# A tile split into two compact pieces, each with its own load and store, in a kernel that gates an image by channel

## The chip, the cores and the metric

One core of one Trainium2 chip. The metric is the device time of one execution in microseconds, median over runs. The kernel before takes 528.1 us.

## The reference

```python
def reference(x, w1d):                       # x: 1 x 384 x 384 x 384 bf16, w1d: 1 value
    g = jnp.einsum("bhwc->bc", x) / (H * W)  # mean of each channel over the image
    ...                                      # k = 1: the "convolution" is s = g * w1d[0]
    s = _sigmoid(s)
    return x * s[:, None, None, :]
```

The output needs the mean of all of x before its first element is certain, yet reading x twice would cost half as much again. The kernel therefore guesses: it takes the gate from 512 of the 147,456 positions, writes x times that gate, sums everything on the way, and at the end compares the true gate with the guess bit by bit in bf16. Only if they differ is everything done again. With the data of this case they don't.

## The kernel before

x is seen as 1152 rows of 128 positions x 384 channels (98.3 KB each), in 18 tiles of 64 rows. Four tiles fit in SBUF (`SLOTS` = 4). All loads of the first four tiles are issued at once; tile k + 4 is loaded into the place of tile k when tile k's store is done. Loads go out on the SyncE queue (except half of tile 0 and all of tile 2), stores on the ScalarE queue. Code cut to what the change touches:

```python
TILE, SLOTS, EARLY, LEAD, FORE, OWN = 64, 4, 4, 8, 32, 16

def dram(view, r0, n):      # n rows of 128 positions; partition p holds n neighbouring positions
    return view[r0 * P : (r0 + n) * P, :].rearrange("(p t) c -> p (t c)", p=P)

# in load: columns i..i+m of an n-row tile
plan.dma(queue, at(place + i, m), dram(x_rows, r0, n)[:, i * C : (i + m) * C], ...)

load(0, TILE, 0, hi=LEAD)                           # 8 rows of tile 0 first: the guess needs 4
plan.dma("sync", w_one[0:1, 0:1], w1d.unsqueeze(0), writes=["w_one"])
load(0, TILE, 0, ("sync", "scalar"), lo=LEAD)       # the other 56 rows, 28 on each queue
load(slot(1), TILE, row0(1))
load(slot(2), TILE, row0(2), ("scalar", "scalar"))
load(slot(3), TILE, row0(3))
# ... sum_early, s_early, TensorE's sums ...
for k in range(n_tiles):
    if k >= SLOTS:
        for i in range(2) if k == SLOTS else () if k < SLOTS + 2 else (k - SLOTS,):
            sum_own(i)                              # VectorE sums 16 of the 64 rows itself
            put(slot(i), TILE, row0(i), parts=None if i else (FORE, TILE - FORE))
        if k == SLOTS:
            pause(slot(k))                          # 3.1 us of ScalarE, behind tile 0's store
        load(slot(k), TILE, row0(k), reads=["pause"] if k == SLOTS else ())
```

Since a tile's partition p holds 64 neighbouring positions, the 8 rows loaded ahead are 128 runs of 6,144 bytes, one every 49,152 bytes of DRAM. `put` gates in place on VectorE (tile 0 in two halves of 32 rows) and then issues one store.

## Time and profile before

| | before |
|---|---|
| median of runs | 528.11 us (527.96 to 529.07) |
| profiled execution | span 526.5 us |
| bytes | 113.25 MB read, 113.25 MB written |
| DMA engines, 10 to 520 us | share 1.00, 434 GB/s |
| VectorE | busy 84% of the span |
| issue of tile 0's store, of tile 1's store, of tile 4's load | 44.1, 68.6, 79.2 us |

A packet is one run of bytes that one DMA engine moves in one piece; each DMA ends with a completion packet of a few bytes on each of the 16 engines (those "under 512 B" below). "Share" is the time that the packets of a stretch took, over the stretch on all 16 engines, so 1.00 means that none was idle. The views count a packet whole in the stretch in which it starts. So over a few microseconds the share swings about 1. "Landing" is the time from the issue of a DMA to its completion.

### The profile page before, as it was taken

To read this page: it belongs to the slowest core of one execution; us is meant where nothing else is said; L and a number is where in the kernel's file an instruction comes from. 1 tells how busy PE (TensorE), PEld (TensorE's weight loads), DVE (VectorE), ACT (ScalarE), POOL (GpSimd) and SP (SyncE) were. 2 spreads that over 40 slices of the span, in tenths; PEclk is the share of its full clock that TensorE was granted. 3 is DMA by queue.
4 is the path that set the end of the run, shared out by engine and by line. 5 is a ranking of instruction groups with operands and counts; after the bars stand their busy time and mean duration, and the time that the engine had idled before them with its cause. 6 is when DMAs were issued, how large, how long until landed. Compare 5 with 4: busy or idle time off the path is not lost.

```text
span 526.5 us, 902 instructions
## 1 busy us (share of the span) xinstructions
PE 180.0 (34%) x648; PEld 0.2 (0%) x2; DVE 440.0 (84%) x78; ACT 5.8 (1%) x5; POOL 0.3 (0%) x6
## 2 busy tenths in 40 slices
PE   2255752043240707061422506070513315070701
PEld 0000000000000000000000000000000000000000
DVE  1869999999996978969696969789696969698795
ACT  1000020000000000000000000000000000000000
POOL 0000000000000000000000000000000000000000
PEclk9996967558585858567575858576675858585765
DMA  9999999999999999999999999999999999999998
GB/s 375 433 459 405 418 448 448 418 418 467 429 418 418 467 429 418 429 459 426 418 429 459 426 418 441 445 429 418 448 437 429 418 459 429 426 418 459 429 426 359
DMA packets 5620, 226.51 MB, mean 430 GB/s; under 512 B 626, under 2 KB 626, under 8 KB 754
## 3 DMA queue, kind: packets, MB, share of 16 engines
q10 hardware_dynamic: 3024, 122.29, 53.7%
q1 hardware_dynamic: 2594, 104.20, 46.0%
q14 instruction: 2, 0.02, 0.0%
HBM read 113.25 MB, written 113.25 MB: 430 GB/s over the span
## 4 chain that ended last, share of the span: by engine, by line
DMA 42%; another core or an unknown queue 27%; DVE 21%; issue 7%; SPq 0%; ACT 0%; DVEq 0%
DMA arena<-in_x_dram 24%; DMA out_dram<-arena 18%; DVE part L338 12%; DVE arena L210 7%; DVE own L345 1%; DVE total L326 0%; SPq L109 0%; DVE own L363 0%; DVE terms L356 0%; ACT arena L488 0%; DVE total L496 0%; DVE total L482 0%; DVE wrong L504 0%; DVE total L324 0%
## 5 line engine op out<-in xcount | busy, mean ns | idle before, releaser
L248 PE MATMUL acc<-arena,ones 128*128 128x512 bf16 x637 | 176.1, 441 | 312.2 <-PEq L292 310.8
L210 DVE TENSOR_TENSOR arena<-arena,s_early 128x24576 bf16<-128x24576 bf16 (+1 forms) x19 | 233.2, 12278 | 11.5 <-PE acc L248 6.5
L338 DVE TENSOR_REDUCE part<-arena 128x384 f32<-128x6144 bf16 x17 | 179.2, 10539 | 56.9 <-DMA arena<-in_x_dram 56.9
L338 DVE TENSOR_REDUCE own<-arena 128x384 f32<-128x6144 bf16 x1 | 10.4, 10435 | 0.6 <-DMA arena<-in_x_dram 0.6
L345 DVE TENSOR_TENSOR own<-own,part 128x384 f32<-128x384 f32 x17 | 9.5, 558 | 0.6
L425 DVE TENSOR_SCALAR w_scaled<-w_all 128x1 f32<-128x1 f32 x2 | 0.2, 152 | 8.0 <-PE w_all L416 8.0
L248 PE MATMUL acc_own<-terms,ones 128*128 128x384 bf16 x3 | 1.4, 479 | 15.3 <-DVE terms L356 15.3
L488 ACT ACTIVATE arena<-total,w_scaled 128x384 bf16<-128x384 f32 x1 | 0.6, 615 | 440.3 <-DVE total L482 440.3
L326 DVE TENSOR_TENSOR total<-total,acc 128x128 f32<-128x128 f32 (+2 forms) x10 | 3.9, 393 | 0.3
L399 ACT ACTIVATE arena<-warm 128x3456 bf16<-128x3456 f32 x1 | 3.1, 3082 | 61.9 <-DMA out_dram<-arena 61.9
L416 PE MATMUL w_all<-w_one,ones 1*128 1x1 bf16 x1 | 0.2, 158 | 9.3 <-DMA w_one<-in_w1d_dram 9.3
L248 PE MATMUL acc<-zeros,ones 128*128 128x512 bf16 x6 | 2.3, 507 | 0.0
L324 DVE COPY total<-acc 128x384 f32<-128x384 f32 x2 | 1.1, 554 | 1.2 <-PE acc L248 1.2
L410 ACT ACT_TABLE_LOAD x1 | 1.3, 1283 | 2.3 <-issue 2.3
L433 DVE MEMSET ones<- 128x128 bf16 x1 | 0.2, 165 | 1.3 <-PEq L611 1.3
L363 DVE TENSOR_TENSOR own<-own,terms 128x384 f32<-128x384 f32 x2 | 1.1, 559 | 0.1
L356 DVE CAST terms<-own 128x384 bf16<-128x384 f32 x3 | 1.1, 359 | 0.1
L496 DVE TENSOR_TENSOR total<-arena,s_early 128x384 f32<-128x384 uint16 x1 | 0.6, 558 | 0.7 <-ACT arena L488 0.7
L448 ACT ACTIVATE s_early<-total,w_scaled 128x384 bf16<-128x384 f32 x1 | 0.6, 614 | 9.8 <-DVE total L326 9.8
L482 DVE TENSOR_TENSOR total<-total,acc_own 128x384 f32<-128x384 f32 x1 | 0.6, 554 | 0.1
L246 PE MATMUL acc<-arena,ones 128*128 128x512 bf16 x1 | 0.6, 608 | 0.0
L504 DVE TENSOR_REDUCE wrong<-total 128x1 f32<-128x384 f32 x1 | 0.6, 553 | 0.0
(10 smaller groups left out, 1.2 us busy)
## 6 DMA issues: line engine op xcount, KB each, us to landing
out_dram<-arena ACTq DMA_DIRECT2D x18, 6144.0 KB, 49.9
arena<-in_x_dram SPq DMA_DIRECT2D x16, 6144.0 KB, 41.8
arena<-in_x_dram ACTq DMA_DIRECT2D x2, 3072.0 KB, 41.5
arena<-in_x_dram ACTq DMA_DIRECT2D x1, 2688.0 KB, 14.0
arena<-in_x_dram SPq DMA_DIRECT2D x1, 2688.0 KB, 21.4
arena<-in_x_dram SPq DMA_DIRECT2D x1, 768.0 KB, 7.8
w_one<-in_w1d_dram SPq DMA_DIRECT2D x1, 0.0 KB
```

Source lines behind the costliest of these rows:

```text
L210: return lambda e: e.tensor_tensor(to_v, v, s_b, ALU.mult)
L246: loaded.append(e.matmul(bank, weights, moving, start=start, stop=stop))
L248: return e.add_instruction(mybir.InstMatmult(name=nc.get_next_instruction_name(), engine=mybir.EngineType.PE, ins=[e.lower_ap(moving), e.l ...
L324: emit = lambda e, part=part, of=of: e.tensor_copy(part, of)
L326: emit = lambda e, part=part, of=of: e.tensor_tensor(part, part, of, ALU.add)
L338: lambda e: e.reduce_sum(to[:], view, axis=mybir.AxisListType.X),
L345: lambda e: e.tensor_tensor(own[:], own[:], part[:], ALU.add),
L356: lambda e, term=term: e.tensor_copy(term, own[:]),
L363: lambda e, term=term: e.tensor_tensor(own[:], own[:], term, ALU.subtract),
L399: lambda e: e.activation(to, warm[:, 0:1].broadcast_to([P, PAUSE * C]), ACT_F.Sigmoid),
L410: lambda e: e.activation(warm[:, 1:2], warm[:, 0:1], ACT_F.Sigmoid),
L448: lambda e: e.activation(s_early[:], total[:], ACT_F.Sigmoid, scale=w_scaled[:, 0:1]),
```

## The change

The intent, as its code suggests: let the first 8 rows be a small tile of their own, contiguous in DRAM (runs of 6,144 bytes that follow each other), which can be loaded alone and, once gated, stored alone, ahead of the other 56 rows. The pause then waits for the last row of tile 0 instead of the first. Cut to its core:

```diff
-    load(0, TILE, 0, hi=LEAD)
+    load(0, LEAD, 0)
     plan.dma("sync", w_one[0:1, 0:1], w1d.unsqueeze(0), writes=["w_one"])
-    load(0, TILE, 0, ("sync", "scalar"), lo=LEAD)
+    load(LEAD, TILE - LEAD, LEAD, ("sync", "scalar"))
...
+    def put_first():
+
+        gated(0, FORE, 0)
+        store(0, LEAD, 0)
+        gated(FORE, TILE - FORE, FORE)
+        store(LEAD, TILE - LEAD, LEAD)
...
-                put(slot(i), TILE, row0(i), parts=None if i else (FORE, TILE - FORE))
+                put(i) if i else put_first()
             if k == SLOTS:
-                pause(slot(k))
+                pause(slot(k) + TILE - 1)
```

(The rest splits `put` into `gated` and `store` and drops two parameters of `load`.)

More of the change, by code (lines that the diff above doesn't have):

```diff
@@ L227, in bass_standalone__channel_attn_eca__vision_kernel, with load @@
     plan = Planner(nc, "a", 70)
-    def load(place, n, r0, queues=("sync",), lo=0, hi=None, reads=()):
-        i, hi = lo, hi or n
-        for queue, m in zip(queues, split(hi - lo, -(-(hi - lo) // len(queues)))):
+    def load(place, n, r0, queues=("sync",), reads=()):
+        i = 0
+        for queue, m in zip(queues, split(n, -(-n // len(queues)))):
             plan.dma(
@@ L378, in join_own, with gated, store, put @@
             )
-    def put(place, n, r0, to=None, parts=None):
-        to, i = place if to is None else to, 0
-        for m in parts or [n]:
-            plan.op(
-                "vector",
-                gate(to + i, place + i, m, s_early),
-                reads=["s_early"] + rows(place + i, m),
-                writes=rows(to + i, m),
-            )
-            i += m
+    def gated(place, n, to):
+        plan.op(
+            "vector",
+            gate(to, place, n, s_early),
+            reads=["s_early"] + rows(place, n),
+            writes=rows(to, n),
+        )
+    def store(place, n, r0):
         plan.final.append(
-            plan.dma("scalar", dram(o_rows, r0, n), at(to, n), reads=rows(to, n))
+            plan.dma("scalar", dram(o_rows, r0, n), at(place, n), reads=rows(place, n))
         )
+    def put(k, to=None):
+        to = slot(k) if to is None else to
+        gated(slot(k), TILE, to)
+        store(to, TILE, row0(k))
+    def put_first():
[3 more added lines that the diff above has]
+        store(LEAD, TILE - LEAD, LEAD)
     def pause(r0):
@@ L471, in bass_standalone__channel_attn_eca__vision_kernel @@
         sum_own(k)
-        put(slot(k), TILE, row0(k))
-    put(slot(last), TILE, row0(last), slot(n_tiles))
+        put(k)
+    put(last, slot(n_tiles))
     sum_own(last)
```

## The prediction

> **What bounds the kernel now.** I read the head of the page and its DMA rows first, because this kernel reads x once and writes it once and does little else.
>
> ```profile
> span 526.5 us, 902 instructions
> PE 180.0 (34%) x648; PEld 0.2 (0%) x2; DVE 440.0 (84%) x78; ACT 5.8 (1%) x5; POOL 0.3 (0%) x6
> ...
> DMA  9999999999999999999999999999999999999998
> ...
> DMA packets 5620, 226.51 MB, mean 430 GB/s; under 512 B 626, under 2 KB 626, under 8 KB 754
> ...
> q10 hardware_dynamic: 3024, 122.29, 53.7%
> q1 hardware_dynamic: 2594, 104.20, 46.0%
> ```
>
> The reader is to see three things. The DMA digit is 9 in every slice but the last. VectorE is busy 84%, a high number, but not a full one. And the two queues split the bytes unevenly: q10 carries the 113.25 MB of stores plus 9.04 MB of early loads (28 rows of tile 0 and the 64 rows of tile 2; one row is 128 x 384 x 2 bytes, 98.3 KB), so q10 is the ScalarE queue and q1 the SyncE queue.
>
> Next I asked for the busy time by stretch, to find the places where the DMA engines are not full:
>
> ```profile
> core 0: us, PE busy (x) PEld busy (x) DVE busy (x) ACT busy (x) POOL busy (x), PEclk, DMA share, GB/s
> 0.00:1.00 1.00, 0.00 (x0) 0.00 (x0) 0.00 (x0) 0.00 (x0) 0.20 (x4) 1.00 0.07 6
> 1.00:2.00 1.00, 0.00 (x0) 0.00 (x0) 0.17 (x1) 0.00 (x0) 0.13 (x2) 1.00 1.07 184
> ...
> 523.00:524.00 1.00, 0.00 (x0) 0.00 (x0) 0.00 (x0) 0.00 (x0) 0.00 (x0) 0.50 1.13 492
> 524.00:525.00 1.00, 0.00 (x0) 0.00 (x0) 0.00 (x0) 0.00 (x0) 0.00 (x0) 0.50 0.15 57
> 525.00:526.00 1.00, 0.00 (x0) 0.00 (x0) 0.00 (x0) 0.00 (x0) 0.00 (x0) 0.50 0.00 0
> ...
> 10.00:520.00 510.00, 179.24 (x646) 0.00 (x0) 438.35 (x72) 4.24 (x3) 0.00 (x0) 0.70 1.00 434
> ```
>
> From 10 to 520 us the engines move 434 GB/s at a share of 1.00. Data starts about 1.3 us into the span and stops at about 524.2 us. So the time is 1.3 us of start, 226.5 MB at 433 GB/s, which is 523.1 us, and some 2.2 us of end: 526.6 against the 526.5 measured. There is no other term. In such a kernel a change helps only if it removes bytes, raises the rate, shortens those 3.5 us, or closes a hole; and it hurts only if it opens one.
>
> Last I read the stretch that the change touches, in the timeline:
>
> ```profile
> 13.61 0.61 ACT L448 ACTIVATE s_early<-total,w_scaled 128x384 bf16<-128x384 f32 x1 [9.82 <-DVE total L326]
> ...
> 31.08 13.03 DVE L210 TENSOR_TENSOR arena<-arena,s_early 128x12288 bf16<-128x12288 bf16 x2 [6.45 <-PE acc L248]
> 44.14 0.36 ACTq L109 DMA_DIRECT2D out_dram<-arena  x1
> ...
> 68.44 10.50 DVE L338 TENSOR_REDUCE part<-arena 128x384 f32<-128x6144 bf16 x1
> ...
> 76.09 3.08 ACT L399 ACTIVATE arena<-warm 128x3456 bf16<-128x3456 f32 x1 [61.87 <-DMA out_dram<-arena]
> ...
> 79.19 0.33 SPq L109 DMA_DIRECT2D arena<-in_x_dram  x1
> ```
>
> Tile 0 is gated in two halves (6.55 us each) from 31.08 us, when TensorE has summed its first 32 rows, to 44.1; its one store is issued there. Tile 1's store follows at 68.6. Tile 0's store is reported at 76.09, the ScalarE pause runs, and SyncE issues the load of tile 4 at 79.19.
>
> **What the Trainium skill says.** All four places are on the page "DMA: Bandwidth & Descriptors". (1) "Where 436 GB/s comes from" gives a fabric ceiling of 435.2 GB/s; the trace agrees, 434 GB/s over 510 us is at it. (2) "Queues, rings and completion order" says that each DMA engine goes round its queues packet by packet, so a queue's share follows its packet size. The trace agrees: from 37.6 to 44.1 us the two queues have 48 and 49 packets, but 1.57 and 1.20 MB. So does the first 8-row load: alternating with 21,504-byte packets it should need 8 packets per engine x (6,144 + 21,504) bytes at 433/16 = 27.06 GB/s, 8.2 us, and lands 7.8 us after issue. (3) "Latency and other measured facts" warns of row pitches at large powers of two; the pitches here are 49,152 bytes before and 6,144 and 43,008 after, none a power of two, and the first stretch already runs near full rate. (4) "Anatomy of one DMA" puts some 2 us of fixed cost per DMA on confirming the write; it fits the 2.2 us at the end here, and the change doesn't touch the last store.
>
> **The change part by part.** *The loads.* Same three pieces of 8, 28 and 28 rows on the same queues, same bytes per partition and packet, only with another pitch in DRAM. From 2 to 10 us the kernel before moves 421 GB/s, so at most 8 x 12/433 = 0.2 us is to be had from a better pattern. The small piece also feeds the early sum, but the first gate waits for TensorE at 31.08 us, and s_early is there at 14.2; a microsecond there buys nothing. Worth: 0 to -0.2 us.
>
> *The data in the early sum.* The 512 positions sampled for s_early are others. If the early gate differed from the true one in any bf16 bit, everything would be done again. I computed both from the inputs: the weight is 0.0012, and the sigmoid stays within 2.1e-6 of 0.5 for the old sample and for the new one, and every value rounds to exactly 0.5 in bf16. No second pass.
>
> *The stores.* One DMA is added: 128 packets of 6,144 bytes and 16 completion packets, while tile 0's other 128 packets shrink to 43,008 bytes; bytes are unchanged. Packets go from 5620 to 5764. The 8-row store is issued after the first gate, at 31.08 + 6.55 = 37.6 us instead of 44.1. It does not start then: the ScalarE queue still holds tile 2's second half, which lands 41.5 us after its issue, so at about 43. Then it alternates with tile 3's load on the SyncE queue, 49,152-byte packets: 8 x (6,144 + 49,152) bytes / 27.06 GB/s = 16.3 us. An 8-row store that alone would take 1.8 us thus ends near 60 us, some 22 us after issue, and the 56-row store waits behind it.
>
> That looks bad for tile 0, but in the same 16.3 us the load gets 8 packets per engine, which is all of tile 3. So tile 3 lands near 62 us instead of at 72, and the 56-row store then has the engines to itself: 5.5 MB / 433 GB/s = 12.7 us. Together: all work issued by 44.1 us is four tiles of loads and one of stores, 31.46 MB, which at 433 GB/s from 1.3 us ends at 74.0 in either order; plus the report, 76, where the trace has 76.09. So the pause and the load of tile 4 stay at 76 and 79 us, within 1 us. The tile that comes early, tile 3, is gated only at 127 us.
>
> *The pause.* It waits for the 56-row store instead of the 64-row one: the same event. Sum of all parts: -0.2 to +0.2 us on 526.5.
>
> **The rivals.** *A hole opens.* If the DMA ran dry before tile 1's store at 68.6 us, the loss would be the gap. For it: VectorE paces the stores there, one each 23.9 us. Against: the work on hand at 68.6 lasts to 74.0, 5.4 us of margin, in any order. Later, one tile's load and store occupy the engines for 29.05 us, a slot's round of four tiles is 116 us, and alone its load, sum, gate and store would need 14.5 + 24 + 14.5 = 53 us; 63 us of slack. At the end the last store takes 21.5 us from its issue at 502.9 to 524.4 or so, 14.5 of them its own: 7 us of backlog. This rival would need to delay something by over 5 us and would make 529 to 533. *The small store helps.* Writes that start 6.5 us sooner could bring everything forward by as much, giving 522 to 526. Against: the engines are full between 37.6 and 44.1, so bytes only change places; and at 435.2 GB/s the bytes alone take 520.5 us, so over 0.8% is out of reach. *A different pattern moves the rate*, by compact loads or small writes: it bears on 1.6 MB, 3.6 us of engine time, so even a 20% change is 0.7 us. *A second pass* would make about 1050 us; the arithmetic above rules it out.
>
> **Range and chances.** The launch adds about 1.5 us to the span, and three runs of the kernel before lie between 527.96 and 529.07. With no net effect, I take its median, 528.1. The range is the spread of the runs plus about 1 us for a shift of phase that I can't work out: 526.9 to 529.4. Chances: faster by over 2% (under 517.5) is beyond the ceiling, 0.005; slower by over 2% needs 10 us of holes, 0.01; within 2%, 0.985.
>
> **What would show it right or wrong.** Right: DMA digits still all 9 and 434 GB/s in the middle, 5764 packets, 8-row store issued near 37.6 us and landing 20 to 25 us later, TensorE's sum of tile 3 starting near 62 us instead of at 72.3, the pause at 76 and tile 4's load at 79, each within 1 us, last data 524 us. Wrong: a stretch under 400 GB/s over 10 us anywhere before the end, tile 1's store issued after the engines ran dry, or a last load landing later than 490 us with the final store standing alone.

## The result, and the profile after

The changed kernel takes 528.23 us (528.13 to 528.59, 6 runs) against 528.12 us (527.90 to 529.07, 6 runs): a ratio of 1.0001, 95% interval 0.9988 to 1.0014. Ratios here are the mean time of one kernel's fast runs over that of the other's fast runs of the same rounds, so they are not quite the ratios of the medians quoted. The change did nothing that can be measured.

The page of the changed kernel, span, DMA share and rate in 40 slices, packets and queues:

```profile
span 527.1 us, 918 instructions
...
DMA  9999999999999999999999999999999999999997
...
DMA packets 5764, 226.51 MB, mean 430 GB/s; under 512 B 642, under 2 KB 642, under 8 KB 898
...
q10 hardware_dynamic: 3168, 122.29, 53.7%
q1 hardware_dynamic: 2594, 104.20, 45.9%
```

Packets go up by the 144 foretold, all on the ScalarE queue (q10: 3024 to 3168); bytes, mean rate and the row of nines stay. Busy time by stretch of the changed kernel, the last two columns being DMA share and GB/s:

```profile
2.00:10.00 8.00, 1.29 (x4) 0.20 (x2) 0.22 (x2) 1.49 (x2) 0.00 (x0) 1.00 1.04 431
10.00:520.00 510.00, 179.43 (x658) 0.00 (x0) 438.21 (x72) 3.70 (x2) 0.00 (x0) 0.68 1.00 433
```

What moved is inside the first 80 us. The timeline of the changed kernel (start, duration, engine, instruction, and in brackets the idle time before it and what ended it):

```profile
29.26 13.03 DVE L210 TENSOR_TENSOR arena<-arena,s_early 128x12288 bf16<-128x12288 bf16 x2 [4.82 <-PE acc L248]
35.85 32.48 ACTq L109 DMA_DIRECT2D out_dram<-arena  x3
...
63.01 7.93 PE L248 MATMUL acc<-arena,ones 128*128 128x512 bf16 x36 [0.63 <-PEq L292]
67.88 10.48 DVE L338 TENSOR_REDUCE part<-arena 128x384 f32<-128x6144 bf16 x1
67.99 0.34 ACTq L109 DMA_DIRECT2D out_dram<-arena  x1
76.50 3.08 ACT L410 ACTIVATE arena<-warm 128x3456 bf16<-128x3456 f32 x1 [62.86 <-DMA out_dram<-arena]
...
79.61 0.33 SPq L109 DMA_DIRECT2D arena<-in_x_dram  x1
```

In the kernel before, TensorE's sum of tile 3 is this line:

```profile
72.28 9.93 PE L248 MATMUL acc<-arena,ones 128*128 128x512 bf16 x35 [9.78 <-PEq L292]
```

The 8-row store is issued at 35.85 us, 8.3 us ahead of the old store. TensorE sums tile 3 from 63.01 us instead of from 72.28. But the pause still starts at 76.5 (76.09 before) and tile 4's load goes out at 79.6 (79.19). Where the early store's head start went is in the list of DMA issues (KB each, us from issue to landing), changed kernel:

```profile
out_dram<-arena ACTq DMA_DIRECT2D x1, 5376.0 KB, 34.2
...
out_dram<-arena ACTq DMA_DIRECT2D x1, 768.0 KB, 27.9
```

The 768 KB store takes 27.9 us, landing at 35.85 + 27.9 = 63.75 us. It first waits behind tile 2's load in its own queue. Asked for the issues from 1.75 to 2.3 us alone, the view gives, for the second half of that load in the changed kernel:

```profile
arena<-in_x_dram ACTq DMA_DIRECT2D x1, 3072.0 KB, 52.0
```

So it lands near 54 us (52.2 us after issue in the kernel before), not at 43. Then the small store meets tile 3's load. The queue rows of the changed kernel from 56 to 58 us:

```profile
q1 hardware_dynamic: 16, 0.79, 91.2%
q10 hardware_dynamic: 16, 0.10, 11.7%
```

Sixteen packets each, but the load's (q1) are eight times as long, so it gets 0.79 MB and the store 0.10. Over the whole stretch from 44.1 to 60 us it looks like this in the changed kernel:

```profile
DMA packets 225, 6.99 MB, mean 440 GB/s; under 512 B 16, under 2 KB 16, under 8 KB 66
...
q1 hardware_dynamic: 113, 5.55, 86.6%
q10 hardware_dynamic: 112, 1.44, 21.2%
```

Kernel before, same stretch:

```profile
q1 hardware_dynamic: 80, 3.93, 60.7%
q10 hardware_dynamic: 95, 2.75, 40.2%
```

Before, the SyncE queue (the load of tile 3; tile 1's data had ended by 44.1) moved 3.93 MB and the ScalarE queue (the rest of tile 2's load and the store) 2.75; now it is 5.55 and 1.44. That is why tile 3 comes 9 us sooner and the store of tile 0 does not. The sums, 6.68 and 6.99 MB, differ by less than one 49 KB packet per engine (0.79 MB), which may be counted on either side of a cut: bytes changed places between two queues, and nothing else.

### The profile page after: what moved, and what is told of

Read it like the earlier page. It is cut to its first block, busy times and chain, and to the rows that moved or that the text cites. A ratio compares the mean times of both kernels' runs of the same rounds, so it can differ in the third digit from the quotient of the medians.

```text
span 527.1 us, 918 instructions
## 1 busy us (share of the span) xinstructions
PE 180.7 (34%) x661; PEld 0.2 (0%) x2; DVE 439.9 (83%) x78; ACT 5.8 (1%) x5; POOL 0.3 (0%) x6
## 2 busy tenths in 40 slices
DMA packets 5764, 226.51 MB, mean 430 GB/s; under 512 B 642, under 2 KB 642, under 8 KB 898
## 3 DMA queue, kind: packets, MB, share of 16 engines
q10 hardware_dynamic: 3168, 122.29, 53.7%
## 4 chain that ended last, share of the span: by engine, by line
DMA 43%; another core or an unknown queue 27%; DVE 21%; issue 7%; SPq 0%; ACT 0%; DVEq 0%
DMA arena<-in_x_dram 24%; DMA out_dram<-arena 18%; DVE part L338 12%; DVE arena L210 7%; DVE own L345 1%; DVE total L326 0%; SPq L109 0%; DVE own L363 0%; DVE terms L356 0%; ACT arena L499 0%; DVE total L507 0%; DVE total L493 0%; DVE wrong L515 0%; DVE total L324 0%
## 5 line engine op out<-in xcount | busy, mean ns | idle before, releaser
L338 DVE TENSOR_REDUCE own<-arena 128x384 f32<-128x6144 bf16 x1 | 10.4, 10432 | 1.0 <-DMA arena<-in_x_dram 1.0
## 6 DMA issues: line engine op xcount, KB each, us to landing
out_dram<-arena ACTq DMA_DIRECT2D x1, 768.0 KB, 27.9
```

Of the source, the lines that this page charges most:

```text
L338: lambda e: e.reduce_sum(to[:], view, axis=mybir.AxisListType.X),
```

## The experiments

My theory: the DMA engines are never idle, so any order of the same bytes takes the same time as long as work is on hand, and small packets at this number are free. Rivals: a gain of the early issue and a loss by the small store cancel; the compact layout matters; VectorE, which spaces the stores at that point, sets the pace. All results were correct; each is quoted beside the kernel before from the same rounds.

**e1_late_small: both stores planned after both gates** (edit on the changed kernel)

```diff
         gated(0, FORE, 0)
-        store(0, LEAD, 0)
         gated(FORE, TILE - FORE, FORE)
+        store(0, LEAD, 0)
         store(LEAD, TILE - LEAD, LEAD)
```

> The changed kernel with its two stores of tile 0 both issued after the second gate (compact loads kept, early issue undone). My theory (the DMA engines are full, so bytes only change places): 528.2 us, within 0.5; the 8-row store is issued near 42.4 instead of 35.9 us and still lands at 62 to 64, because either way it starts about 43 us and alternates with 49,152-byte load packets. Rival (the early issue is a real gain that pays for the extra small store): 529 to 534, later by up to the 6.5 us that the store loses.

Measured 528.12 us (before 528.30; ratio 0.9998, 0.9982 to 1.0015). But the edit failed of its purpose: the profile has the first store issued at 36.56 us, right after the first gate. The plan lets ScalarE wait for what its store reads, which is the first gate alone, and moving the line does not change that. So this run is only a repeat of the changed kernel, and says nothing of the early issue. The next one does, since there ScalarE must wait for the second gate first.

**e2_big_first: the 56-row store ahead of the 8-row one**

```diff
         gated(0, FORE, 0)
-        store(0, LEAD, 0)
         gated(FORE, TILE - FORE, FORE)
         store(LEAD, TILE - LEAD, LEAD)
+        store(0, LEAD, 0)
...
-                pause(slot(k) + TILE - 1)
+                pause(slot(k))
```

> The changed kernel with the 56-row store ahead of the 8-row one, both after the second gate. My theory: 528.2 us within 0.5. The order inside the queue moves again: 43,008-byte packets alternate with tile 3's 49,152-byte ones, so tile 3 lands near 70 to 72 us (TensorE's sum of it starts there, not at 63), the 8-row store lands last, near 76, and tile 4's load is still issued at 79 to 80. Rival (the 8-row store blocking the 56-row one costs something): faster than the changed kernel by 1 us or more.

Measured 528.38 us (before 528.30; ratio 1.0003, 0.9987 to 1.0020). The timeline of this kernel:

```profile
42.98 25.34 ACTq L109 DMA_DIRECT2D out_dram<-arena  x3
...
72.22 10.13 PE L248 MATMUL acc<-arena,ones 128*128 128x512 bf16 x33 [10.31 <-PEq L292]
77.12 3.08 ACT L410 ACTIVATE arena<-warm 128x3456 bf16<-128x3456 f32 x1 [63.47 <-DMA out_dram<-arena]
...
80.23 0.33 SPq L109 DMA_DIRECT2D arena<-in_x_dram  x1
```

The first store is 7.1 us later than in the changed kernel, tile 3's sum starts at 72.2 again instead of at 63.0, and tile 4's load moves by 0.6 us. The time does not change. So neither the early issue nor the place of the small store is worth anything that these runs can tell (the interval is 0.2% wide on either side), and a gain and a loss of these two that cancel are ruled out, since this run takes both away.

**e3_strided_split: the stores split, the loads and the layout as before** (edit on the kernel before, in `put`, with its lines joined here; `parts` is set for tile 0 only)

```diff
             i += m
-        plan.final.append(
-            plan.dma("scalar", dram(o_rows, r0, n), at(to, n), reads=rows(to, n))
-        )
+            if parts:
+                lo, hi = (0, LEAD) if i < n else (LEAD, n)
+                plan.final.append(
+                    plan.dma("scalar", dram(o_rows, r0, n)[:, lo * C : hi * C],
+                             at(to + lo, hi - lo), reads=rows(to + lo, hi - lo)))
+        if not parts:
+            plan.final.append(
+                plan.dma("scalar", dram(o_rows, r0, n), at(to, n), reads=rows(to, n)))
```

(The pause waits for the last row, as in the changed kernel.)

> The kernel before with its tile layout (8 rows as a part of 64, pitch 49,152 bytes in DRAM, loads as before), but with tile 0's store split into 8 and 56 rows, the first issued after the first gate. So the store half of the change without the compact pieces. My theory: 528.1 us within 0.5, 8-row store landing near 62 to 64 us as in the changed kernel, since the pitch doesn't matter. Rival (the compact layout is what keeps the small store cheap, or compact loads gain what the store loses): 1 us or more slower than the changed kernel.

Measured 528.37 us (before 528.30; ratio 1.0002, 0.9985 to 1.0019). The 8-row store is issued at 36.58 us and lands 26.7 us later, at 63.3. Within the 0.2% of these runs, the layout in DRAM doesn't matter at this size.

**e4_small_runs, e10_runs_12k, e11_runs_3k: many more small packets.** In the changed kernel every load and store is cut into runs of 8 rows (6,144 bytes), then 16 (12,288 bytes, tile 0 left alone) and 4 (3,072 bytes). Loads and stores use the same view, with as many DMAs as the changed kernel:

```diff
+    def runs(view, r0, place, n):
+        far = view[r0 * P : (r0 + n) * P, :].rearrange(
+            "(a p t) c -> p a (t c)", p=P, t=LEAD)          # 8; 16 and 4 in the others
+        near = at(place, n).rearrange("p (a m) -> p a m", a=n // LEAD)
+        return far, near
...
-            plan.dma("scalar", dram(o_rows, r0, n), at(place, n), reads=rows(place, n))
+            plan.dma("scalar", *runs(o_rows, r0, place, n), reads=rows(place, n))
```

(In e4 tile 0's 56 rows were loaded as 32 and 24 rather than 28 and 28, to be whole runs.)

> The disputed cost 70 times over: every load and store of the changed kernel moves 6,144-byte runs (each 8 rows compact in DRAM), with as many DMAs as the changed kernel. My theory says that 6,144-byte packets run at the full rate: 528 to 531 us; the packets under 8 KB become nearly all, about 37,500. Rival (a small packet costs something, hidden in 1.6 MB of it): a cost of 0.02 us per packet and engine would be 18,432 x 2 / 16 x 0.02 = 46 us, so 575; anything over 533 would speak for it, and the cost per packet can be read off.

> Second point of the small-run line: runs of 12,288 bytes in tiles 1 to 17, tile 0 as in the changed kernel; about 18,700 packets, 12,900 more than the changed kernel, 808 per engine. If each packet costs 5.2 ns of its engine (10.4 us of the 6,144-byte kernel over 31,744/16 extra packets): 4.2 us, 532.4 us. Rival (the 10 us came of the other pattern in DRAM or of a knee, not of the number of packets): nearer 528 or 538.

> Third point: runs of 3,072 bytes everywhere, about 74,400 packets, 68,600 more than the changed kernel, 4,288 per engine. At 5.2 ns each: 22.3 us, 550.5 us. Rival as for the second point: not on the line (under 543 or over 558).

| run length | packets | median us | before, same rounds | over the changed kernel's 528.23 | extra packets per engine | ns per packet |
|---|---|---|---|---|---|---|
| as changed | 5,764 | 528.23 | 528.12 | | | |
| 12,288 (e10) | 18,692 | 532.55 | 528.06 | 4.3 | 808 | 5.3 |
| 6,144 (e4) | 37,508 | 538.62 | 528.30 | 10.4 | 1,984 | 5.2 |
| 3,072 (e11) | 74,373 | 548.31 | 528.06 | 20.1 | 4,288 | 4.7 |

The last column is the difference in time over the extra packets of one of the 16 engines. The engines are full in all three, at a lower rate. DMA share and GB/s from 10 to 520 us, first e4:

```profile
10.00:520.00 510.00, 177.43 (x651) 0.00 (x0) 430.52 (x54) 3.33 (x2) 0.00 (x0) 0.69 1.01 425
```

For e10 and e11 the same stretch gives 430 and 416 GB/s. Here my expectation for e4, the full rate, was wrong: a packet does cost something, and 533 us was my own limit for saying so. The points lie nearly on a line in the number of packets, which speaks against the layout and for a cost per packet, though a layout effect that grew in step with it would look the same. Applied to the change: 128 more data packets are 8 per engine, 8 x 5.2 ns = 0.04 us. The rival's cost exists, and is far too small to have hidden a gain.

**e5_wait4, e6_wait10, e7_wait21, e8_before_wait10: a later store of tile 1.** VectorE gets a useless sum over 6, 16 or 32 rows ahead of tile 1's own sum; the fourth does it with 16 rows in the kernel before:

```diff
+    def linger(k, n):                      # result is overwritten
+        view = at(slot(k) + TILE - n, n).rearrange("p (t c) -> p c t", t=n)
+        plan.op("vector", lambda e: e.reduce_sum(part[:], view, axis=...X), ...)
...
+                if i == 1:
+                    linger(1, 6)            # 16; 32; 16
                 sum_own(i)
```

> The changed kernel with an extra VectorE sum of 6 rows of tile 1 (thrown away; result right) ahead of tile 1's own sum, about 4 us (10.5 us x 6/16), so tile 1's store is issued near 72 instead of 68.0 us. My theory: the work issued by then (four loads, one store, 31.46 MB) keeps the DMA engines busy to 74.0, so nothing is lost: 528.2 us within 0.5. Rival (VectorE paces the stores in this stretch, and later ones follow): the whole 4 us, 532.

> The same with 16 rows, 10.5 us, tile 1's store at 78.5 us. My theory: the engines run dry at 74.0, 4.5 us are lost for good: 532.7 us (531.7 to 533.7). Rival (VectorE paces): 538.7. Rival (slack anywhere): 528.2.

> The same with 32 rows, 21 us, tile 1's store at 89 us. My theory: the engines run dry at 74.0 until tile 4's load, issued at 79.6, brings work; that load and the store of tile 1 last to about 109, and tile 2's store comes at 112.9, another 2 to 4 us of hole: 535 to 539 us in all. Rival (VectorE paces): 549.

> The kernel before with the same 16 extra rows, tile 1's store near 79.1 us. My theory: the margin is the work on hand, which the change leaves as it was: 5.1 us lost from 528.1, 533 us (532 to 534), the same as the changed kernel within 1 us. Rival (the split and the early small store give or take margin): over 1.5 us apart from the changed kernel with the same wait.

| | tile 1's store issued | median us | range |
|---|---|---|---|
| before, same rounds | | 528.19 | 527.82 to 531.70 |
| e5, 4 us | 72.2 | 528.58 | 528.28 to 530.16 |
| e6, 10 us | 78.6 | 534.35 | 534.23 to 537.62 |
| e8, 10 us, kernel before | 79.0 | 535.37 | 534.25 to 538.88 |
| e7, 21 us | 89.1 | 547.73 | 544.59 to 550.90 |

This chip was less steady than the others; its runs of the kernel before reach 531.7. Still, the first 4 us cost nothing that these runs can tell, and the next 6 cost about as many. e5 is within my range; e6 and e8 miss theirs (531.7 to 533.7, and 532 to 534) by 0.7 and 1.4 us, on the slow side. DMA share and GB/s for e6 show where the engines ran dry:

```profile
72.00:74.00 2.00, 0.00 (x0) 0.00 (x0) 2.00 (x1) 0.00 (x0) 0.00 (x0) 1.00 1.44 624
74.00:76.00 2.00, 0.00 (x0) 0.00 (x0) 2.00 (x1) 0.00 (x0) 0.00 (x0) 1.00 0.10 43
76.00:78.00 2.00, 0.00 (x0) 0.00 (x0) 2.00 (x1) 0.00 (x0) 0.00 (x0) 0.54 0.00 0
78.00:80.00 2.00, 0.00 (x0) 0.00 (x0) 2.00 (x2) 0.97 (x1) 0.00 (x0) 0.50 0.93 393
```

Two more views of e6 settle when the work on hand ends. First the queue's row from 73.5 to 75 us, then all packets from 75 to 79.4 us:

```profile
q10 hardware_dynamic: 16, 0.69, 105.9%
```

```profile
DMA packets 16, 0.00 MB, mean 0 GB/s; under 512 B 16, under 2 KB 16, under 8 KB 16
```

The last 16 data packets start from 73.5 us on (the last at 74.5) and take 1.6 us each (1.059 x 1.5 us), so the work ends between 75.1 and 76.1 us, one to two microseconds after the prediction's 74.0. Then there are only completion packets, until the data of the store issued at 78.64 start at 79.5. That is about 4 us with nothing to move. From 70 to 140 us e6 moves 400 GB/s where the changed kernel moves 434, which is 70 x 34/434 = 5.5 us; the median run lost 6.1 (534.35 - 528.23). (The profile is of the slowest of the five runs, 537.62; much of its further loss is at the end, as in e12 below.) In e8, the kernel before, no data packet starts between 75 and 79.8 us either, so the margin is about the same with and without the change; the two medians are 1.0 us apart, within their ranges.

e7 missed: 547.7 against 535 to 539, close to the rival's 549. The timeline of e7 shows a cause that I had overlooked:

```profile
89.06 0.34 ACTq L109 DMA_DIRECT2D out_dram<-arena  x1
89.44 3.08 ACT L420 ACTIVATE arena<-warm 128x3456 bf16<-128x3456 f32 x1 [75.71 <-DVE arena L210]
92.55 54.94 SPq L109 DMA_DIRECT2D arena<-in_x_dram  x3
```

The pause stands behind tile 1's store in ScalarE's program, so a late store holds up the pause, and with it tile 4's load, which I had counted on to fill the hole.

**e12_wait21_pause_first: the same with the pause planned ahead of tile 1's store** (edit on e7)

```diff
                 put(i) if i else put_first()
-            if k == SLOTS:
-                pause(slot(k) + TILE - 1)
+                if k == SLOTS and i == 0:
+                    pause(slot(k) + TILE - 1)
```

> The changed kernel with 21 us of extra VectorE work ahead of tile 1's store, as before, but with the pause planned ahead of that store on the ScalarE queue, so that tile 4's load no longer sits behind it. In the last such run the load was issued at 92.6 us, after the store at 89.1, where I had reckoned with 79.6. If that order is what made it 547 instead of 535 to 539: 536 to 540 here, load issued near 79.6, the dry stretch ending near 80. Rival (VectorE's delay itself is what costs): 545 to 550 again.

Measured 542.82 us (539.07 to 543.74; before 528.06, 527.81 to 528.75). This misses too: it lies between my 536 to 540 and the rival's 545 to 550. Tile 4's load goes out at 79.81 us, and data move again from 80.8. So the order was a cause, worth some 5 us (547.7 - 542.8, on two chips). The remaining loss of 14.6 us (542.82 - 528.23) is more than the first hole, 75.2 or later to 80.8. Where it lies can be read in part from the stretches of e12:

```profile
80.00:82.00 2.00, 0.00 (x0) 0.00 (x0) 2.00 (x1) 0.00 (x0) 0.00 (x0) 0.50 1.28 393
...
95.00:140.00 45.00, 9.51 (x36) 0.00 (x0) 44.93 (x7) 0.00 (x0) 0.00 (x0) 0.61 0.97 404
```

The changed kernel, for the second of them:

```profile
95.00:140.00 45.00, 10.25 (x36) 0.00 (x0) 44.44 (x6) 0.00 (x0) 0.00 (x0) 0.61 1.01 437
```

From 70 to 140 us e12 moves 367 GB/s where the changed kernel moves 434, which is 10.8 us. That takes in the first hole; a second shortage, 404 against 437 GB/s from 95 to 140 us, in which the work on hand runs out before the data of tile 2's store, issued at 112.6, begin (e7's expectation had named this one); and packets that take longer after a hole (in 80 to 82 us, share 1.28 for 393 GB/s, 2.6 us each instead of 1.8). Afterwards the rate is the usual one: 434 GB/s from 200 to 400 us, against 435. Most of the rest of this profiled run (543.5 us), some 3 us, lies at the end, where a few engines drain late:

```profile
536.00:539.00 3.00, 0.00 (x0) 0.00 (x0) 0.00 (x0) 0.00 (x0) 0.00 (x0) 0.50 0.12 52
539.00:542.00 3.00, 0.00 (x0) 0.00 (x0) 0.00 (x0) 0.00 (x0) 0.00 (x0) 0.50 0.04 16
```

A dry stretch thus costs more than its own length here. Why packets take longer after it, and why the engines then end apart, is left open.

**e9_no_pause: tile 4's load right behind tile 0's stores**

```diff
-            if k == SLOTS:
-                pause(slot(k) + TILE - 1)
-            load(slot(k), TILE, row0(k), reads=["pause"] if k == SLOTS else ())
+            load(slot(k), TILE, row0(k))
```

> The changed kernel without the 3.1 us ScalarE pause ahead of tile 4's load (the change moved which store it waits for). My theory: the engines have tile 1's store on hand until 88.5 us, so a load issued at 76.5 instead of 79.6 us changes nothing: 528.2 us within 0.5. Rival (the pause, or its place behind the last piece of tile 0, sets the pace of the later tiles): over 1 us either way.

Measured 529.17 us (528.18, 529.85, 528.49 and 530.83; before 528.06, 527.81 to 528.75): ratio 1.0030, 1.0008 to 1.0051. My expectation was within 0.5 and fails narrowly. Two of four runs are as fast as with the pause, two are 1.6 and 2.6 us slower, and the profile caught a fast one (load at 76.61 us, no hole), so it cannot show what the slow ones lack. The pause may steady the kernel, but four runs do not show it: the kernel before, with its pause, also had runs of 529.9 and 531.7 on another chip. It is not a part of the change, which leaves its start within half a microsecond of where it was.

No run pointed to a version faster than both kernels. 226.51 MB at 433 GB/s are 523.1 of the 526.5 us, and nothing tried here lowered bytes or raised the rate.

## Why the prediction was right

- **The bound.** Right: bytes over rate fill nearly the whole span of the changed kernel too (433 GB/s from 10 to 520 us), and the time is 528.23 against the predicted 528.1. But the 2.2 us of end are not quiet, as the sum has them: packets are counted where they start, and in the kernel before the last one starts at 524.1 us and ends at 525.9. The prediction's 520.5 us are an estimate from the ceiling that it takes from the Trainium skill; no run tested that ceiling, and it leaves 523.1 - 520.5 = 2.6 us or 0.5%, not the 0.8%.
- **The compact loads, 0 to -0.2 us.** The stretch from 2 to 10 us went from 421 to 431 GB/s, and w1d's value, the load behind the small piece, released TensorE at 8.71 instead of 9.28 us. Over the first 10 us it is 375 instead of 356 GB/s (e1 and e2, also compact, 378 and 375; e3, with the old layout, 358), which is 0.4 us and twice the gain allowed for. By 40 us the two kernels have moved as much (423 and 422 GB/s), and in the time it is lost in the noise.
- **No second pass.** Right; there is none in the trace.
- **The small store's detour.** Right that it would gain nothing and let tile 3 pass; one step of the way there was wrong. "Tile 2's second half, which lands 41.5 us after its issue, so at about 43": the 41.5 is the median of two DMAs, the two halves, and asked for one by one they took 30.7 and 52.2 us. So the store starts on most engines near 54.8 us, some 11 us later than I had it, alternates with tile 3's load only until the last packets of that end near 61 us, and has the engines to itself for the rest: landing 63.75 instead of near 60, and 27.9 us after its issue instead of the 20 to 25 that were to show the prediction right. The alternation itself is what the counts of 16 and 16 packets show. Its share of the time is shorter than the 16.3 us worked out, since the load was further on by then. Tile 3 was to land near 62, and its sum starts at 63.01, so there the error hardly shows. Issue was put at 37.6 and came at 35.85, because TensorE began 0.6 us sooner and took 7.05 us instead of 8.31 for the rows that the first gate waits for (29.26 - 22.21 against 31.08 - 22.77); e3, with the old layout, has its gate at 29.99, and e1 and e2, with the new one, at 29.97 and 29.92, so the layout is not the main reason, and I did not look further.
- **The pause and tile 4's load, 76 and 79 within 1 us.** 76.50 and 79.61. That the same bytes end at about the same time in either order is shown by e6 and e8 (75.1 to 76.1 us, and 75.1 to 75.5). The 74.0 itself was too early by one to two microseconds, and the 2 us added for the report too long by as much: in the kernel before the last completion packet is at 75.7, and the pause starts at 76.09. That the sum of the two came out right is luck.
- **The margin of 5.4 us.** Confirmed only as lying between 4 us of delay (free) and 10 us (6.1 us lost), and as about equal in both kernels. With the work ending at 75.1 or later and 0.9 us from issue to first data, both as in e6, an estimate for the changed kernel is 75.1 - 0.9 - 68.0 = 6.2 us.
- **Readings that do not hold.** The check on the first 8-row load, 7.8 us against 8.2, is a coincidence: in the first 3 us the view shows 72 packets of the SyncE queue and 3 of the other, so they did not yet alternate. Of the 48 packets counted from 37.6 to 44.1 us, 16 are completion packets; the clean sign of alternation is the 16 and 16 from 56 to 58 us. And the gate at 127 us is tile 4's; tile 3 is gated at 103.2, still long after its load.
- **A sign of being wrong that came up.** A stretch under 400 GB/s over 10 us: from 60 to 70 us the changed kernel shows 392. It means nothing, since the kernel before has 398 from 130 to 140; so short a stretch depends on which long packets start in it. From 40 to 80 us both show 423.
- **Small packets.** The prediction allowed up to 0.7 us for any change of pattern. The measured cost is 0.04 us by the packet count; only the expectation of e4, that 6,144-byte packets run at the full rate even by the ten thousand, was wrong.

The rival of the small store helping was refuted by e2, which stores later and is as fast, and that of a hole by the row of nines (e6, with its hole of 4 us, shows a 7 there).

## What to carry to other kernels

When the DMA engines are full from end to end, issuing a transfer sooner only decides whose bytes wait; ask what the queue has on hand at the moment, not how early a store can be issued. Work out the time at which the issued bytes run out (bytes over rate; here good to one or two microseconds) and compare it with the next issue: the difference is about the delay that costs nothing. A small store is no express either: it waits its turn in its own queue and then gives up a long packet for each short one, and 0.8 MB took 27.9 us here. A median landing time over two DMAs of one queue is not the landing of either. And before reading a short stretch of a view, find out whether it counts a packet where it starts or where it ends.

## What the Trainium skill lacked or had wrong

- "DMA: Bandwidth & Descriptors", section "Why small descriptors are slow (HBM only)": it gives two costs, about 3 cycles of overhead per packet and 32 bytes of descriptor metadata, and speaks of sizes around 256 bytes. With beats of 32 bytes and the 850 MHz of "Where 436 GB/s comes from" the two would be, as an estimate, 4 cycles or 4.7 ns; the runs agree with 4.7 to 5.3 ns per packet and engine. What the section lacks is that this counts far above 256 bytes: runs of 3,072 bytes still cost 3.8% (548.31 us).
- The same page, "Rules for kernel authors": for the most bandwidth it asks for 128 partitions and 1 MiB per DMA; that row does not speak of the length of the runs. DMAs of 6 MB and 128 partitions ran at 434, 430, 425 and 416 GB/s with runs of 49,152, 12,288, 6,144 and 3,072 bytes.
- The same page, "Queues, rings and completion order": it tells of the alternation by packet, but not what it does to a small transfer. Here one packet is one run of up to 49,152 bytes in the trace's count, and a store of 6,144-byte packets got 0.10 MB in the 2 us in which a load of 49,152-byte ones got 0.79.
- The same page, "Where 436 GB/s comes from": its sentence that for transfers between HBM and SBUF the HBM side (about 358 GB/s) binds does not hold with one core running: reads and writes of HBM together made 434 GB/s here. (The same note calls a measured 425 near the fabric's rate.)
- No page has it: what the engines lose after they have run dry once. In e12 it was 14.6 us for a first hole of about 5: a second shortage, packets of 2.6 instead of 1.8 us after the hole, and a few engines that ended late.
